# A fused linear-attention and MLP kernel: the loads of ScalarE's Gelu table are no longer written by hand

## The chip, the cores and the metric

The kernel runs on one core of a Trainium2 chip. A core has five engines with a queue each: TensorE (PE, matrix products into PSUM), ScalarE (ACT, activation functions and copies), VectorE (DVE, elementwise work), GpSimd (POOL) and SyncE (SP), which here mostly start transfers. The metric is the device time of one execution in microseconds. The time shown is a median of three runs; one further execution was taken with the hardware profiler, and all rows of the trace come from that one.

## The reference

There are two parts, one behind the other. The first is a gated linear attention: a state per batch and head decays row by row with `alpha`, takes in `k` times `v`, and is read with `q`. The second is an MLP with the tanh form of Gelu over all tokens.

```python
# q, k, v, alpha: (4, 8, 768, 48), float32
for t in range(S):
    state = alpha[:, :, t, :, None] * state + np.einsum('bhd,bhe->bhde', k[:, :, t], v[:, :, t])
    y[:, :, t] = np.einsum('bhd,bhde->bhe', q[:, :, t], state)
...
# x: (3072, 384), w_in: (384, 2048), w_out: (2048, 384)
h = x @ w_in
c = np.float32(np.sqrt(2.0 / np.pi))
g = 0.5 * h * (1.0 + np.tanh(c * (h + 0.044715 * h * h * h)))
return (g @ w_out).astype(np.float32)
```

## The kernel before

The 768 rows of a sequence are cut into six chunks of 128, the four batches into two pairs. That makes twelve pieces, "pairs" in the code, each of one chunk and two batches. Every piece goes through attention and then through the MLP.

**Attention of a piece.** ScalarE takes the logarithm of alpha (`la`, line 222). TensorE sums it along the chunk with a triangular matrix (`cum`, lines 232 and 234). ScalarE makes the exponentials of the sum and of its negative (`b` and `binv`, line 249) and of the chunk's end (`bend`, line 245). DVE multiplies `q` and `k` with them (`qp`, `kp`, line 257), TensorE transposes both (`qkT_ps`, line 268), DVE copies the transposes out of PSUM (line 278; ScalarE does some of the first two pieces). TensorE multiplies them (`at`, line 290) and DVE applies the causal mask (`atm`, line 297). TensorE makes the piece's share of the state (`kv`, line 307), which DVE adds to the state (the carry, lines 322 and 324), and the output `yps` (lines 336 and 339). That is copied out as `x` by ScalarE or DVE (line 346), transposed on TensorE (line 353) and copied into `xT` by DVE (line 357).

**MLP of a piece.** Layer 1 makes sixteen tiles `hT` of 128 x 256, each from three matmuls (line 363). ScalarE takes the Gelu of each into `gT` (line 369). Layer 2 makes two tiles `acc` of 128 x 384, each from sixteen matmuls (line 377), ScalarE or DVE copies them out as `ot` (line 384), and SyncE stores them (line 389). `hT` and `acc` share four PSUM buffers (tag `ff`): the next `hT` can be computed only when an older one has gone through its Gelu or an older `acc` has been copied.

**The order.** The program is a list of tasks, each with a kind, a modelled cost per engine, a priority, its dependencies and the buffers it takes. `Scheduler.order` (lines 49 to 120) walks through modelled time and puts the task that can start first, with the smaller priority within 60 ns, on its engine. Each engine's queue runs in that order, and an instruction that waits holds up all behind it. The MLP tasks of all pieces form one stream in a fixed order; the attention of the next pieces is put between them. A few matmuls of zeros (`idle`, line 190) are put in gaps of TensorE in the first 60 us of the plan.

**The function tables.** [...] Logarithm and exponential are in the set that the kernel calls `LN_EXP = 6`, the copies need no set of their own, and the kernel calls the set for the Gelu `GELU = 0`. The planner keeps track of the set: a task that needs another one gets 1,290 ns (`W["table"]`) added to its earliest start (line 99), and `t.load` is set to the number of the set (line 117). While the instructions are written, `run` puts a load ahead of each such task with `act_set` (lines 179 to 183), so those loads have line 181 in the trace. Independently, the compiler puts in loads of its own where it finds that an activation needs one; those have the line of that activation.

The tasks `ln` and `exp` need the first set, `gelu` the second. The Gelus of a piece are kept together, and the logarithm of a later piece waits for the last of them (lines 533 to 536), so the set changes about twice per piece.

Of the kernel before, what the change touches and what calls it, by code (L numbers as in the profile page):

```python
# [11 lines left out]
LN_EXP, GELU = 6, 0  # L12
# [117 lines left out]
class _Kernel:  # L130
# [407 lines left out]
    def run(self):  # L538
        nc = self.nc
        self.tasks()  # L540
        self.act_set(LN_EXP)
        nc.vector.memset(self.zero, 0.0)  # L542
        nc.vector.memset(self.ones, 1.0)
        first = [lambda: make_upper_triangular(nc, self.ut_h, val=1.0, diag=True), lambda: make_identity(nc, self.ident)]
        for i in range(self.BUFS["la"]):
            for n in ("la", "qp", "kp"):
                nc.vector.memset(self.ring[n][i][:, :, :, self.D:64], 0.0)
        for b in range(self.B):
            for i in range(2):
                nc.vector.memset(self.state[b][i], 0.0)  # L550
        order = self.s.order()
        self.plan = order
        gap = 0
        for t in order:
            if t.load is not None:
                self.act_set(t.load)
            t.emit(t.engine)
            if t.kind == "load" and t.engine == "POOL" and first:
                first.pop(0)()
                if not first:  # L560
                    nc.vector.tensor_copy(self.ut, self.ut_h)
# [30 lines left out]
```

## Time and profile before

| | before |
|---|---|
| median of three runs | 205.69 us (204.83 to 205.86) |
| the profiled execution | 205.91 us |
| its span, first to last instruction | 204.1 us |
| TensorE, busy | 185.2 us, 91% of the span |
| ScalarE, busy | 151.0 us, 74% |
| DVE, busy | 105.6 us, 52% |
| GpSimd, busy | 61.3 us, 30% |
| table loads, line 181 | 20, together 25.7 us |
| table loads, line 369 | 10, together 12.8 us |
| granted TensorE clock, mean over the span | 0.979 |

In rows of a group, the line and engine come first, then the operation, its output and input with their shapes, and how many there were; after the first bar the busy time in us and the mean of one in ns, after the second the idle time of the engine just before them and who ended it. In rows in order of time, start and duration in us come first, and a number in square brackets is the idle time before, with the instruction that ended it. TensorE's matmuls are pipelined and their ends are modelled: the duration of a row can reach over the start of the next one. "PEclk" or a clock is the share of the full TensorE clock that was granted.

### The profile page before, as it was taken

Reading aid. Unit: us, or ns where it says so; the run is one execution under the profiler, and the core shown is the slowest. Engines: PE = TensorE matmul, PEld = TensorE weight load, DVE = VectorE, ACT = ScalarE, POOL = GpSimd, SP = SyncE. Lnnn points to the kernel's source line nnn. Section 1 sums busy time; section 2 is a strip of 40 time slices with the busy share of each in tenths; the row PEclk is TensorE's granted clock in tenths of the full one; section 3 lists DMA queues with packets and bytes.
Section 4 is the critical chain, followed back from the end, with each engine's and each line's share of the span. In section 5 each row is a group of like instructions: output and inputs, shape, how many; then the busy total and the mean of one; then the engine's idle time right before and its main releaser. Section 6 shows DMA issues by size and latency. Waiting matters only on the chain.

```text
span 204.1 us, 4664 instructions
## 1 busy us (share of the span) xinstructions
PE 185.2 (91%) x1925; PEld 133.7 (65%) x1927; DVE 105.6 (52%) x219; ACT 151.0 (74%) x317; POOL 61.3 (30%) x63
## 2 busy tenths in 40 slices
PE   7786489999899989989989989989989989989992
PEld 2343358866578667767767767767777776676861
DVE  6373642037987394494494593594593550650000
ACT  2635767971789698798798798798798888883740
POOL 7983653464655664422410510000000000000000
PEclk9999958999999999999999999999999999999998
DMA  7999999999999999997980580200200200200202
GB/s 137 166 226 172 200 202 220 177 175 238 226 221 154 182 235 186 181 244 145 161 189 2 130 181 2 80 0 3 77 0 3 77 3 0 79 3 6 75 0 77
DMA packets 37941, 24.68 MB, mean 121 GB/s; under 512 B 27904, under 2 KB 34560, under 8 KB 37920
## 3 DMA queue, kind: packets, MB, share of 16 engines
q0 software_dynamic: 32400, 19.27, 67.2%
q1 hardware_dynamic: 5520, 5.11, 8.3%
q8 instruction: 15, 0.25, 0.6%
q14 instruction: 6, 0.05, 0.1%
HBM read 25.17 MB, written 4.72 MB: 146 GB/s over the span
## 4 chain that ended last, share of the span: by engine, by line
PE 70%; ACT 16%; DMA 6%; POOL 4%; issue 1%; DVE 1%; POOLq 0%; DVEq 0%
PE acc L377 31%; PE hT L363 27%; DMA k<-in_k_dram 6%; ACT L369 6%; ACT L181 6%; PE at L290 2%; PE yps L339 2%; ACT ot L384 2%; ACT gT L369 2%; PE cum L232 2%; PE yps L336 2%; PE xT_ps L353 2%; POOL q L202 1%; PE qkT_ps L268 1%; PE kv L307 1%
## 5 line engine op out<-in xcount | busy, mean ns | idle before, releaser
L363 PE MATMUL hT<-xT,w_in 128*128 128x256 bf16 x576 | 74.9, 278 | 8.1 <-ACT gT L369 7.9
L377 PE MATMUL acc<-w_out,gT 128*128 128x384 bf16 x384 | 68.4, 326 | 0.0
L369 ACT ACTIVATE gT<-hT 128x256 bf16<-128x256 f32 x192 | 62.0, 388 | 6.1 <-PE hT L363 5.6
L363 PEld LDWEIGHTS <-w_in 128*128 128x128 bf16 x576 | 54.6, 99 | 17.5 <-issue 9.4
L377 PEld LDWEIGHTS <-gT 128*128 128x128 bf16 x384 | 36.0, 98 | 20.4
L297 DVE TENSOR_TENSOR atm<-at,ut 128x512 bf16<-128x512 f32 x48 | 30.8, 684 | 8.1 <-PE at L290 7.0
L257 DVE TENSOR_TENSOR qp<-q,b 128x768 bf16<-128x768 f32 x12 | 11.5, 958 | 32.8 <-ACT b L249 32.8
L181 ACT ACT_TABLE_LOAD x20 | 25.7, 1283 | 1.1 <-PEq L576 0.7
L384 ACT COPY ot<-acc 128x384 f32<-128x384 f32 x18 | 8.6, 478 | 16.9 <-PE acc L377 16.7
L202 POOL DMA_DIRECT2D v<-in_v_dram x12 | 13.8, 1153 | 17.6 <-PE xT_ps L353 9.7
L346 ACT CAST x<-yps 128x384 bf16<-128x384 f32 x22 | 10.5, 478 | 11.5 <-PE yps L339 11.3
L202 POOL DMA_DIRECT2D a<-in_alpha_dram x11 | 12.7, 1153 | 20.7 <-ACT la L222 13.4
L278 DVE COPY qkT<-qkT_ps 128x1024 bf16<-128x1024 bf16 (+1 forms) x21 | 13.3, 673 | 7.6 <-PE qkT_ps L268 7.6
L357 DVE COPY xT<-xT_ps 128x384 bf16<-128x384 bf16 x24 | 8.5, 356 | 16.6 <-PE xT_ps L353 16.5
L202 POOL DMA_DIRECT2D q<-in_q_dram x12 | 14.0, 1163 | 9.9 <-DVE qp L257 4.2
L202 POOL DMA_DIRECT2D k<-in_k_dram x12 | 13.8, 1152 | 4.8 <-DVE stmp L322 2.3
L249 ACT ACTIVATE b<-cum 128x768 bf16<-128x768 f32 x12 | 9.7, 810 | 7.4 <-PE cum L234 7.4
L222 ACT ACTIVATE la<-a 128x768 f16<-128x768 f32 x12 | 10.1, 843 | 4.1 <-DMA a<-in_alpha_dram 4.0
L369 ACT ACT_TABLE_LOAD x10 | 12.8, 1283 | 0.1
L257 DVE TENSOR_TENSOR kp<-k,binv 128x768 bf16<-128x768 f32 (+1 forms) x14 | 11.6, 837 | 2.4 <-DMA k<-in_k_dram 2.4
L190 PE MATMUL idle<-zero 128*128 128x512 bf16 x37 | 11.3, 432 | 1.3 <-DVE zero L542 1.2
L324 DVE TENSOR_TENSOR st<-stmp,bend 64x192 bf16<-64x192 f32 x32 | 11.3, 353 | 1.7
(43 smaller groups left out, 167.2 us busy)
## 6 DMA issues: line engine op xcount, KB each, us to landing
q<-in_q_dram POOLq DMA_DIRECT2D x12, 384.0 KB, 12.6
k<-in_k_dram POOLq DMA_DIRECT2D x12, 384.0 KB, 12.7
out_dram<-ot SPq DMA_DIRECT2D x24, 192.0 KB, 1.9
a<-in_alpha_dram POOLq DMA_DIRECT2D x11, 384.0 KB, 12.6
v<-in_v_dram POOLq DMA_DIRECT2D x12, 192.0 KB, 12.6
w_in<-in_moe_w_in_dram POOLq DMA_DIRECT2D x4, 384.0 KB, 10.1
w_out<-in_moe_w_out_dram POOLq DMA_DIRECT2D x4, 384.0 KB, 14.7
a<-in_alpha_dram SPq DMA_DIRECT2D x1, 384.0 KB, 4.1
```

The costliest lines, as they stand in the source:

```text
L181: nc.scalar.add_instruction(mybir.InstLoadActFuncSet(name=nc.get_next_instruction_name(), act_func_set_id=i, engine=mybir.EngineType.Activ ...
L190: self.nc.tensor.matmul(ps, self.zero[:, 0:self.C], self.zero, start=True, stop=True)
L202: (nc.sync if e == "SP" else nc.gpsimd).dma_start(t.rearrange("t b h d -> t (b h) d"), src)
L257: self.nc.vector.tensor_tensor(u[n + "p"][:, lo:hi, :, 0:self.D], u[n][:, lo:hi], u["b" if n == "q" else "binv"][:, lo:hi], op=ALU.mult)
L278: self.copy(e)(t, u.pop(("T_ps", i, which)))
L297: self.nc.vector.tensor_tensor(u["atm", i][:, o], u["at", i][:, o], self.ut[:, None, :].to_broadcast([self.C, self.H // 2, self.C]), op=AL ...
L324: nc.vector.tensor_tensor(new[ps, :, fs], acc, u["bend"][ps, i, :, None].to_broadcast([64, H // 2, D]), op=ALU.mult)
L346: self.copy(e)(x, u["y", i].rearrange("t h d -> t (h d)"))
L363: self.nc.tensor.matmul(h, self.w_in[:, j, nt * self.C:(nt + 1) * self.C], self.xT[c][:, j, lo:hi].rearrange("p g t -> p (g t)"), start=j ...
L369: return lambda e: self.nc.scalar.activation(self.gT[c % self.NG][:, nt, lo * self.C:hi * self.C], f.pop(("h", c, lo, nt)), AF.Gelu_apprx_ ...
L377: self.nc.tensor.matmul(f["acc", c, b], self.gT[c % self.NG][:, nt, b * self.C:(b + 1) * self.C], self.w_out[:, nt, :], start=nt == 0, sto ...
L384: self.copy(e)(f["ot", c, b], f.pop(("acc", c, b)))
```

## The change

In the loop of `run`, a load is now written only where the task that follows needs the Ln/Exp set. The load ahead of the first Gelu of a stretch is not written any more. The load at the very start (line 541) stays. Two assignments that nothing reads, `self.plan` and `gap`, go as well. The planner, the costs that it uses, the buffers and the transfers are not touched.

```diff
@@ -549,11 +549,9 @@
             for i in range(2):
                 nc.vector.memset(self.state[b][i], 0.0)
         order = self.s.order()
-        self.plan = order
-        gap = 0
         for t in order:
-            if t.load is not None:
-                self.act_set(t.load)
+            if t.load == LN_EXP:
+                self.act_set(LN_EXP)
             t.emit(t.engine)
             if t.kind == "load" and t.engine == "POOL" and first:
                 first.pop(0)()
```

## The prediction

> **What bounds the kernel now.** I read the page of the profile first (the load on each engine, then the costliest groups), then the list of who waits for whom, and then the instructions in order of time around the table loads, ScalarE (ACT) beside TensorE (PE).
>
> ```profile
> span 204.1 us, 4664 instructions
> PE 185.2 (91%) x1925; PEld 133.7 (65%) x1927; DVE 105.6 (52%) x219; ACT 151.0 (74%) x317; POOL 61.3 (30%) x63
> ...
> L181 ACT ACT_TABLE_LOAD x20 | 25.7, 1283 | 1.1 <-PEq L576 0.7
> ...
> L369 ACT ACT_TABLE_LOAD x10 | 12.8, 1283 | 0.1
> ```
>
> TensorE is busy for 91% of the span, so whatever is done on ScalarE can give at most what TensorE now waits for. There are thirty table loads. Twenty carry line 181, the loads written by hand: one at the start, ten for Gelu, nine back to Ln/Exp. Ten more carry line 369, the Gelu activation itself, where the kernel writes no load: the compiler puts those in. So each change to Gelu is paid twice. The next view is the list of waits, the row of TensorE waiting for ScalarE's Gelu:
>
> ```profile
> PE hT L363 <- ACT gT L369: 7.9, 9, 2.1
> ```
>
> Of the 18.9 us in which TensorE is not busy (204.1 - 185.2), 7.9 us in nine waits are for the first Gelu output of a stage. Here is one steady stage, ScalarE in order of time (start, duration, line), then TensorE:
>
> ```profile
> 85.49 0.48 ACT L384 COPY ot<-acc 128x384 f32<-128x384 f32 x1 [0.39 <-PE acc L377]
> 85.98 1.28 ACT L181 ACT_TABLE_LOAD   x1
> 87.27 1.28 ACT L369 ACT_TABLE_LOAD   x1
> 88.57 2.50 ACT L369 ACTIVATE gT<-hT 128x256 bf16<-128x256 f32 x8
> ...
> 92.47 0.48 ACT L346 CAST x<-yps 128x384 bf16<-128x384 f32 x1
> ```
>
> ```profile
> 87.16 0.49 PE L363 MATMUL hT<-xT,w_in 128*128 128x256 bf16 x3
> 87.67 0.40 PE L290 MATMUL at<-qkT 64*128 64x128 bf16 x8
> 88.00 0.34 PE L307 MATMUL kv<-v,kp 128*128 128x96 bf16 x4
> 89.00 0.49 PE L363 MATMUL hT<-xT,w_in 128*128 128x256 bf16 x3 [0.66 <-ACT gT L369]
> 89.33 0.33 PE L307 MATMUL kv<-v,kp 128*128 128x96 bf16 x4
> 89.50 1.15 PE L363 MATMUL hT<-xT,w_in 128*128 128x256 bf16 x9
> ```
>
> The four hT buffers in PSUM (tag `ff`) are full, the fifth hT needs the first Gelu, and that stands behind two loads. TensorE waits 0.66 us, although the loads together are 2.56 us: most of them is covered by the matmuls at 87.16 to 88.34.
>
> **The change part by part.** It takes away the ten hand-written Gelu loads; ten loads at line 369 and ten at line 181 should be left. ScalarE loses 10 x 1.283 = 12.8 us of work. The list of tasks, its order, the buffers and all transfers stay: the planner ran before with one load of 1,290 ns per change and does so still. The two assignments that go (`self.plan`, `gap`) make no instruction.
>
> The price of one load is read from starts: 85.98 to 87.27 is 1.29, 87.27 to 88.57 is 1.30, so a load costs its 1.283 us and nothing after it, and it starts 0.01 us after the copy before it. [...]
>
> With every first Gelu 1.28 us earlier, what does TensorE gain in each stage? It gains no more than its wait. The wait as listed counts from the modelled end of the matmul before; by starts it is longer. Four kv matmuls take 89.33 to 89.50 = 0.17 before the next one starts, so the waiting hT could have started at 88.00 + 0.17 = 88.17, not at 89.00: 0.83. The Gelu will release it at 89.00 - 1.28 = 87.72, which is 0.45 before TensorE gets there, so all 0.83 goes. Five stages (85.98, 101.04, 116.09, 131.14, 146.20) are alike: 5 x 0.83 = 4.15. The others:
>
> ```profile
> 73.05 0.49 PE L363 MATMUL hT<-xT,w_in 128*128 128x256 bf16 x3
> 74.12 1.14 PE L363 MATMUL hT<-xT,w_in 128*128 128x256 bf16 x9 [0.57 <-ACT gT L369]
> ...
> 162.93 0.40 PE L290 MATMUL at<-qkT 64*128 64x128 bf16 x8
> 164.27 1.80 PE L363 MATMUL hT<-xT,w_in 128*128 128x256 bf16 x15 [0.94 <-ACT gT L369]
> ```
>
> At 74.12: three hT take 0.33 by starts (89.00 to 89.33), so 73.38 was possible: 0.74. At 164.27: eight `at` take 0.33 (87.67 to 88.00), so 163.26 was possible: 1.01, and the stage that starts at 176.13 is the same, 1.00. Both lie under 1.28. The eight stages give 0.74 + 4.15 + 2.01 = **6.90 us**. Their lower bound is the listed idle time, 0.57 + 5 x 0.66 + 2 x 0.94 = 5.75.
>
> One change to Gelu gives nothing, the one at 55.31:
>
> ```profile
> 56.59 1.28 ACT L369 ACT_TABLE_LOAD   x1
> 57.89 0.66 ACT L369 ACTIVATE gT<-hT 128x256 bf16<-128x256 f32 x2
> ```
>
> ```profile
> 57.14 0.82 PE L363 MATMUL hT<-xT,w_in 128*128 128x256 bf16 x6
> ```
>
> Its hT only starts at 57.14 and TensorE has no Gelu wait there; I cost it at 0. It also shows that the compiler's load doesn't wait for the matmul as its activation does: it began at 56.59. So the load left over takes the removed one's place in time.
>
> The first change to Gelu needs care, because of the clock:
>
> ```profile
> 23.33 1.28 ACT L181 ACT_TABLE_LOAD   x1
> 24.61 1.28 ACT L369 ACT_TABLE_LOAD   x1
> 25.91 1.66 ACT L369 ACTIVATE gT<-hT 128x256 bf16<-128x256 f32 x5
> ```
>
> ```profile
> 23.69 0.52 PE L307 MATMUL kv<-v,kp 128*128 128x96 bf16 x8
> 26.34 0.80 PE L363 MATMUL hT<-xT,w_in 128*128 128x256 bf16 x3 [2.13 <-ACT gT L369]
> ```
>
> Stretches of TensorE by their granted clock (from:to, length, busy, clock, share of the DMA engines, GB/s):
>
> ```profile
> 25.00:25.10 0.10, 0.00 (x0) 0.63 1.31 205
> ...
> 31.80:31.90 0.10, 0.10 (x5) 0.73 1.44 388
> ...
> 202.50:203.00 0.50, 0.00 (x0) 0.52 0.00 0
> ```
>
> Here the wait is longer than a load, so TensorE restarts at 26.34 - 1.28 = 25.06 and still waits about a microsecond, from 23.69 + 2 x 0.17 = 24.03 to 25.06. The clock halves at 25.03 (0.63 over that tenth of a microsecond) and comes back at 31.85. From 26.34 to 31.85 TensorE works without a break at half clock: 5.51 us for 2.76 us of full-clock work. What the earlier restart is worth depends on when the clock returns, which the trace of before can't show. Bounds: it returns at 31.85 as before, and 25.06 to 31.85 holds 6.79 / 2 = 3.40 of work instead of 2.76: 0.64 gained. Or it never drops, because the gap is shorter: 1.28 + 2.76 = 4.04. Between: the three changes of the clock, 25.03, 31.85 and 202.52, lie 6.82 and 170.67 apart, 2 and 50 steps of 3.41. If the clock is judged at such steps, the first step of the slow stretch (25.03 to 28.44) held 1.31 of idle time and was not enough, and the second (28.44 to 31.85), busy throughout, was. With the restart at 25.06 already the first is full, and the clock returns at 28.44: 3.38 / 2 = 1.69 of the work is done by then, the other 1.07 by 29.51 instead of 31.85: **2.34 us**. I take this, since the whole of the first step is then like the whole of the second; the drop itself at 25.03 lies before the new restart, and nothing before it changes.
>
> [...]
>
> **What could be late next.** DVE, in the steady stages, and the loads in the first third:
>
> ```profile
> 90.52 0.35 DVE L324 TENSOR_TENSOR st<-stmp,bend 64x192 bf16<-64x192 f32 x1
> 91.01 1.29 DVE L297 TENSOR_TENSOR atm<-at,ut 128x512 bf16<-128x512 f32 x2
> ...
> 92.96 0.36 DVE L322 TENSOR_TENSOR stmp<-kv,st 64x192 f32<-64x192 f32 x1
> ```
>
> ```profile
> 94.56 0.33 PE L336 MATMUL yps<-st,qkT 128*128 128x96 bf16 x4
> ```
>
> ```profile
> 45.52 0.85 ACT L222 ACTIVATE la<-a 128x768 f16<-128x768 f32 x1
> 49.41 0.48 ACT L384 COPY ot<-acc 128x384 f32<-128x384 f32 x1 [3.05 <-PE acc L377]
> ```
>
> DVE is busy until 90.52 + 0.35 = 90.87, so the masks at 91.01 and the carry behind them can come only 0.14 earlier, while TensorE comes 0.83 earlier. The next y (94.56) needs the carry's read of kv (ends 93.32): 94.56 - 0.83 = 93.73 against 93.18, a reserve of 0.55. I cost it at 0. The Ln at 45.52 is the one whose input may land too late once TensorE is some 2 us ahead, but behind it ScalarE has 3.05 us of idle time, so this too is 0. The Ln/Exp load and its Ln follow the y matmuls of the same stage and move with TensorE.
>
> **The sum.** The profiled execution took 205.91 us (204.1 span and 1.8 around it), 0.22 above the median of 205.69, so inside the spread of the three runs (204.83 to 205.86 is 1.03 wide). 205.91 - 6.90 - 2.34 = 196.67, say **196.7 us**, 4.4% under the median. With the lower bounds 205.91 - 5.75 - 0.64 = 199.5; with the upper ones 205.91 - 6.90 - 4.04 = 195.0.
>
> **The rivals.**
>
> The slow clock lasts as long as before. Then the first change gives 0.64: 205.91 - 6.90 - 0.64 = 198.4. For it: steps of 6.82 fit the three changes of the clock as well (1 and 25). and a clock judged at other moments in another execution could do the same. Against: the stretch from 28.44 to 31.85, without a pause, is more than enough of a busy step, and the new first half equals it. Chance 0.26.
>
> Another wait takes over: the carry binds y. That needs the reserve of 0.55 to be gone, for instance if y waits for the carry's end rather than its read. At worst DVE lets six stages (74 to 149) gain 0.14 each instead of 0.74 to 0.83, 4.05 less: 196.7 + 4.05 = 200.7. Chance 0.06.
>
> All nine removed loads on the chain count in full:
>
> ```profile
> PE 70%; ACT 16%; DMA 6%; POOL 4%; issue 1%; DVE 1%; POOLq 0%; DVEq 0%
> PE acc L377 31%; PE hT L363 27%; DMA k<-in_k_dram 6%; ACT L369 6%; ACT L181 6%; PE at L290 2%; PE yps L339 2%; ACT ot L384 2%; ACT gT L369 2%; PE cum L232 2%; PE yps L336 2%; PE xT_ps L353 2%; POOL q L202 1%; PE qkT_ps L268 1%; PE kv L307 1%
> ```
>
> The chain has line 181 with 6%, about nine times 1.28 = 11.5 us: 205.91 - 11.5 = 194.4. Against: beside the loads TensorE has its own work, and a chain shorter by 1.28 hands over to it after 0.83. Chance 0.05.
>
> A removed load frees more than its own 1.283 us. If a wait after it went too, the first change would lose its whole pause (24.03 to 26.34, 2.31) and with it the slow clock, 2.76: 205.91 - 6.90 - 5.07 = 193.9. No row shows such a wait. Chance 0.03. [...]
>
> Nothing is removed: the hand-written load was what let the compiler do with one, and it places two now. The time stays at 205.9. Against: its load at line 369 begins 0.01 us behind the hand-written one and is the last before the Gelu, so it pays no heed to it. Chance 0.03.
>
> Slower: without the hand-written load the compiler chooses a set for the Gelu stretch that lacks the copy of `x` (line 346, at 92.47 between the Gelus), and loads twice around it, 2.57 us. TensorE runs ahead of ScalarE by the four hT buffers, 4 x 0.33 = 1.31, so 1.26 of it is lost; the time is worse than before from 9.24 / 1.26 = 7.3 such places on. With one in each of the nine stages 196.7 + 11.3 = 208.0. Against: the set in use there is already the compiler's own choice and the copies run without a load. Chance 0.03.
>
> **How the numbers follow.** The forecast has 0.54; its own range, from the bounds of the eight waits and of small shifts of the clock's steps, is 196.0 to 198.0. The range for 8 in 10 takes in the rival of the clock and most of the way to the bounds: 195.2 to 199.2. A difference of under 0.5% (1.0 us, the spread of the three runs) can't be told from no change. Faster than that are the forecast and the first four rivals, 0.94; the same, 0.03; slower, 0.03.
>
> **What would show it.** Line 181 with ten loads, line 369 with ten; ScalarE 12.8 us less busy. No Gelu wait of TensorE in the stages from 71 us on, and those stages shorter by 0.74 to 1.0. One wait of about 0.9 us near 24, then half clock for 3.4 us instead of 6.8. Wrong would be: loads at other lines; waits of TensorE for DVE at `yps` in place of the Gelu ones; a slow stretch that still ends near 31.9 or doesn't occur.

## The result, and the profile after

The changed kernel takes 197.60 us (median of four runs, 195.95 to 198.04), the kernel before 205.78 (204.83 to 205.93): a ratio of 0.9597 with a 95% interval of 0.9534 to 0.9661, 8.2 us less. The forecast was 196.7, its range 195.2 to 199.2. The profiled execution of the changed kernel took 195.95 us with a span of 194.2, the fastest of the four.

The page of the changed kernel: engines, chain, and the groups with the loads.

```profile
span 194.2 us, 4654 instructions
PE 184.1 (95%) x1925; PEld 133.1 (69%) x1927; DVE 105.7 (54%) x219; ACT 139.7 (72%) x307; POOL 61.4 (32%) x63
...
PE 84%; DMA 6%; POOL 4%; ACT 2%; DVE 1%; issue 1%; POOLq 0%; DVEq 0%
...
L181 ACT ACT_TABLE_LOAD x10 | 12.8, 1283 | 0.9 <-PEq L574 0.7
...
L369 ACT ACT_TABLE_LOAD x10 | 12.8, 1283 | 0.2
```

Ten loads are gone, and they are those of line 181. ScalarE's share of the chain falls from 16% to 2%: TensorE is now followed back nearly without a break. ScalarE lost 11.3 us of busy time and not 12.8, because the 192 Gelus are busy for 1.4 us longer (63.4 instead of 62.0): Gelus that stand back to back overlap (eight took 2.50 us at 88.57 in the kernel before, where one takes 0.38), and ScalarE now waits for an hT between them 19 times instead of 15.

The same steady stage as in the prediction, ScalarE and then TensorE in order of time, and TensorE's only wait for a Gelu in the whole program:

```profile
81.54 0.48 ACT L384 COPY ot<-acc 128x384 f32<-128x384 f32 x1 [0.39 <-PE acc L377]
82.04 1.28 ACT L369 ACT_TABLE_LOAD   x1
83.33 1.21 ACT L369 ACTIVATE gT<-hT 128x256 bf16<-128x256 f32 x4
```

```profile
84.05 0.34 PE L307 MATMUL kv<-v,kp 128*128 128x96 bf16 x4
84.23 0.49 PE L363 MATMUL hT<-xT,w_in 128*128 128x256 bf16 x3
84.56 0.33 PE L307 MATMUL kv<-v,kp 128*128 128x96 bf16 x4
```

```profile
PE hT L363 <- ACT gT L369: 0.8, 1, 0.8
```

The hT that waited now starts 0.18 after the kv matmuls before it. To see where the time went, the same instruction is looked up in both traces, first in the kernel before, then in the changed one: the start of the first layer 2, of a `cum` in three later stages, and of the last-but-one long run of layer 2. "Ahead by" in the table behind them is the start in the kernel before less the start in the changed one.

```profile
39.22 3.41 PE L377 MATMUL acc<-w_out,gT 128*128 128x384 bf16 x20
82.81 0.32 PE L232 MATMUL cum<-la,ut_h 128*128 128x384 f16 x1
158.08 0.32 PE L232 MATMUL cum<-la,ut_h 128*128 128x384 f16 x1
172.96 0.33 PE L232 MATMUL cum<-la,ut_h 128*128 128x384 f16 x1
184.59 5.36 PE L377 MATMUL acc<-w_out,gT 128*128 128x384 bf16 x32
```

```profile
36.01 3.41 PE L377 MATMUL acc<-w_out,gT 128*128 128x384 bf16 x20
78.87 0.32 PE L232 MATMUL cum<-la,ut_h 128*128 128x384 f16 x1
150.02 0.32 PE L232 MATMUL cum<-la,ut_h 128*128 128x384 f16 x1
163.90 0.33 PE L232 MATMUL cum<-la,ut_h 128*128 128x384 f16 x1
174.64 5.36 PE L377 MATMUL acc<-w_out,gT 128*128 128x384 bf16 x32
```

| up to | ahead by | gained there | the prediction's term |
|---|---|---|---|
| 39.22 | 3.21 | 3.21 | 2.34 for the first change |
| 82.81 | 3.94 | 0.73 | 0 for the change near 55, 0.74 for the next |
| 158.08 | 8.06 | 4.12 in five stages | 4.15 |
| 172.96 | 9.06 | 1.00 | 1.01 |
| 184.59 | 9.95 | 0.89 | 1.00 |

Behind 184.59 nothing changes. The first 39 us gave more than the term, and a part of that isn't due to the change. TensorE's wait for `kp`, which stands behind a transfer of k (DVE begins `kp` when that has landed, at 21.67 before and 20.78 after), and the first Gelu, first before, then after:

```profile
22.29 0.87 PE L268 MATMUL qkT_ps<-ident,kp 128*128 128x128 bf16 x8 [1.25 <-DVE kp L257]
```

```profile
21.40 0.86 PE L268 MATMUL qkT_ps<-ident,kp 128*128 128x128 bf16 x8 [0.63 <-DVE kp L257]
...
24.16 0.80 PE L363 MATMUL hT<-xT,w_in 128*128 128x256 bf16 x3 [0.85 <-ACT gT L369]
```

The transposes of k start 0.89 earlier in this execution, ahead of any Gelu. Without that 3.21 - 0.89 = 2.32 is left for the first change. The clock of TensorE in the changed kernel, by tenths of a microsecond:

```profile
24.10:24.20 0.10, 0.04 (x1) 0.72 1.27 200
27.50:27.60 0.10, 0.10 (x2) 0.72 1.35 207
```

It fell at 24.14 and came back at 27.56, 3.42 us later; in the kernel before the slow stretch was 6.82 us long (25.03 to 31.85). One step of 3.4 us stands in place of two. That is the case on which the 2.34 was worked out. But the other three runs of the changed kernel have a mean clock of 0.983, 0.979 and 0.978 instead of 0.991, and took 197.3 to 198.0. That is the mean of two slow steps: the kernel before, with two, has 0.979, in which a slow stretch behind its last matmul counts too (from 202.52 to the end at 204.1). Whether that explains the 0.9 us between forecast and median was the first question for the experiments.

### The profile page after: what moved, and what is told of

Read it like the earlier page. It is cut to its first block, busy times and chain, and to the rows that moved or that the text cites. A ratio compares the mean times of both kernels' runs of the same rounds, so it can differ in the third digit from the quotient of the medians.

```text
span 194.2 us, 4654 instructions
## 1 busy us (share of the span) xinstructions
PE 184.1 (95%) x1925; PEld 133.1 (69%) x1927; DVE 105.7 (54%) x219; ACT 139.7 (72%) x307; POOL 61.4 (32%) x63
## 4 chain that ended last, share of the span: by engine, by line
PE 84%; DMA 6%; POOL 4%; ACT 2%; DVE 1%; issue 1%; POOLq 0%; DVEq 0%
PE hT L363 33%; PE acc L377 32%; DMA k<-in_k_dram 6%; PE qkT_ps L268 5%; PE at L290 4%; PE yps L339 2%; PE kv L307 2%; PE xT_ps L353 2%; PE cum L232 2%; PE yps L336 2%; POOL q L202 1%; PE cum L234 1%; POOL w_in L210 1%; DVE kp L257 1%; ACT L369 1%
## 5 line engine op out<-in xcount | busy, mean ns | idle before, releaser
L363 PE MATMUL hT<-xT,w_in 128*128 128x256 bf16 x576 | 73.8, 275 | 1.1 <-ACT gT L369 0.8
L369 ACT ACTIVATE gT<-hT 128x256 bf16<-128x256 f32 x192 | 63.4, 386 | 8.5 <-PE hT L363 7.3
L363 PEld LDWEIGHTS <-w_in 128*128 128x128 bf16 x576 | 53.7, 98 | 9.4 <-issue 1.7
L257 DVE TENSOR_TENSOR qp<-q,b 128x768 bf16<-128x768 f32 x12 | 11.5, 958 | 33.1 <-ACT b L249 33.1
L190 PE MATMUL idle<-zero 128*128 128x512 bf16 x37 | 12.4, 468 | 1.3 <-DVE zero L542 1.2
L181 ACT ACT_TABLE_LOAD x10 | 12.8, 1283 | 0.9 <-PEq L574 0.7
L369 ACT ACT_TABLE_LOAD x10 | 12.8, 1283 | 0.2
L324 DVE TENSOR_TENSOR st<-stmp,bend 64x192 bf16<-64x192 f32 x32 | 11.3, 353 | 1.7
## 6 DMA issues: line engine op xcount, KB each, us to landing
out_dram<-ot SPq DMA_DIRECT2D x24, 192.0 KB, 1.9
v<-in_v_dram POOLq DMA_DIRECT2D x12, 192.0 KB, 12.9
```

The lines of the kernel that those rows point to most:

```text
L181: nc.scalar.add_instruction(mybir.InstLoadActFuncSet(name=nc.get_next_instruction_name(), act_func_set_id=i, engine=mybir.EngineType.Activ ...
L190: self.nc.tensor.matmul(ps, self.zero[:, 0:self.C], self.zero, start=True, stop=True)
L257: self.nc.vector.tensor_tensor(u[n + "p"][:, lo:hi, :, 0:self.D], u[n][:, lo:hi], u["b" if n == "q" else "binv"][:, lo:hi], op=ALU.mult)
L324: nc.vector.tensor_tensor(new[ps, :, fs], acc, u["bend"][ps, i, :, None].to_broadcast([64, H // 2, D]), op=ALU.mult)
L363: self.nc.tensor.matmul(h, self.w_in[:, j, nt * self.C:(nt + 1) * self.C], self.xT[c][:, j, lo:hi].rearrange("p g t -> p (g t)"), start=j ...
L369: return lambda e: self.nc.scalar.activation(self.gT[c % self.NG][:, nt, lo * self.C:hi * self.C], f.pop(("h", c, lo, nt)), AF.Gelu_apprx_ ...
```

## The experiments

The theory: a stage gains what TensorE waited there and no more (6.90 us in eight stages), and the first change gives something between 0.64 and 4.04, by how the slow stretch of the clock falls. The rivals: every removed load on the chain counts in full; the gain is mainly one of the clock; a load by hand is dear in itself. All times below are medians, with the kernel before run on the same chip beside them.

### The load back at the first change only

```diff
             if t.load == LN_EXP:
                 self.act_set(LN_EXP)
+            elif t.load == GELU:
+                changes += 1
+                if changes == 1:
+                    self.act_set(GELU)
```

> The hand-written Gelu load is put back ahead of the first change to Gelu alone, so the first change is as in the kernel before and the other nine are as in the changed kernel. My account (a stage gains its wait and no more): 205.8 - 6.90 = 198.9, between 197.9 and 199.9 as the slow clock falls; stages of 14.23 us in place of 15.05. The rival that every removed load on the chain counts in full: 205.8 - 8 x 1.28 = 195.5. The rival that nearly all came from the slow clock near 25 us: about 204.

Measured: 198.76 against 205.62, ratio 0.966 (0.9613 to 0.9706). The nine changes behind the first give 6.86 us by the medians; the term was 6.90. The interval leaves room for 6.0 to 8.0, so the agreement to 0.04 is luck, and the tighter test of the term is the sum of the differences in the traces above, 0.73 + 4.12 + 1.00 + 0.89 = 6.74. The rival that counts the loads, 195.5, lies outside the interval (197.7 to 199.6), and so does the one by the clock alone. In the profiled execution (199.27 us) the first pause is back, 1.6 us, and the only Gelu wait left:

```profile
PE hT L363 <- ACT gT L369: 1.6, 1, 1.6
```

### The load back at all changes but the first

```diff
-                if changes == 1:
+                if changes > 1:
```

> The hand-written Gelu load is put back ahead of all changes but the first. My account: the first change alone gives 0.64 (slow clock as long as before) to 2.34 (one step shorter): 203.5 (202.4 to 205.2). Together with the kernel that has it only at the first change this should make up the whole gain of 8.2: 6.9 there and 1.3 to 2.3 here.

Measured: 204.18 against 205.15, ratio 0.9932 (0.9901 to 0.9963). The first change alone gives 0.97 us by the medians and 1.4 by the ratio, with an interval of 0.8 to 2.0. Its twelve runs spread from 201.69 to 204.86, and the mean clock goes with them: 201.7 and 202.0 at 0.998 and above, 203.2 at 0.992, 203.5 to 204.3 at 0.983, 204.5 to 204.9 at 0.980. Two slow steps are the common case, and in it the first change gives about 1 us. By the medians 6.86 + 0.97 = 7.83; the whole change gave 8.18 in its first runs, 7.90 and 8.38 in the two repeats below.

### The changed kernel again, twice

> The changed kernel again. My account: its runs fall in groups by how long the slow clock lasts near 24 us, one step of 3.4 us (195.9 as in the profiled execution, clock 0.991) or two (198, clock 0.979), with up to 0.9 us more by when the transfer of k lands; nothing between the stages of 71 and 190 us moves. If the spread comes from elsewhere, the clock of the runs doesn't go with their span.

> The changed kernel beside the kernel with added matmuls, on the same chip: 197.2, clock 0.983 in most runs (two steps of the slow clock).

Measured: 197.25 (195.45 to 198.00) against 205.15, and 197.17 (196.63 to 197.97) against 205.55; ratios 0.9611 (0.9573 to 0.9649) and 0.9601 (0.9574 to 0.9628). All sixteen runs of the changed kernel fall into groups by mean clock:

| mean clock | runs | time |
|---|---|---|
| 0.991 to 0.998 | 3 | 195.45 to 196.63 |
| 0.983 | 8 | 196.92 to 197.57 |
| 0.978, 0.979 | 5 | 197.73 to 198.04 |

Two steps of 3.41 us at half clock (0.50 in the rows below) in 195.5 us are a mean clock of 1 - 3.41 / 195.5 = 0.983. So the execution that was profiled first, with one step, is one of the rare ones; the usual one has two. The traces of the two repeats bear this out: the one with a mean of 0.998 has no slow step near 24 us (1.00 from 18 to 35), the one with 0.983 has two. Here are the two (from:to, length, busy, clock), and TensorE's first wait for a Gelu in the same execution:

```profile
23.15:26.56 3.41, 3.08 (x30) 0.50 1.29 203
26.56:29.97 3.41, 3.41 (x24) 0.50 1.31 203
```

```profile
24.82 0.80 PE L363 MATMUL hT<-xT,w_in 128*128 128x256 bf16 x3 [0.33 <-ACT gT L369]
```

Here the clock fell at 23.15, ahead of the wait. The first slow step holds the wait, and a second one followed. In the execution with one step the clock fell at 24.14, when the wait was all but over (24.16).

### Matmuls of zeros in the pauses, in both kernels

Ahead of the transposes of q, of those of k and of kv of the second piece, TensorE gets work whose results nobody reads, where it waits in any case.

```diff
+            second = u is self.p[0, 1] and i == 0
+            if second and which == "q":
+                idle = self.tile("yk", [C, 512], F32, "idle")
+                for _ in range(4):
+                    nc.tensor.matmul(idle, self.zero[:, 0:C], self.zero, start=True, stop=True)
...
+            for _ in range(6 if second and which == "k" else 0):
+                nc.tensor.transpose(ps[:, 0, 0, :], self.ident, self.ident)
...
+            for _ in range(5 if u is self.p[0, 1] and i == 0 else 0):
+                nc.tensor.matmul(kv.rearrange("t p d -> t (p d)"), self.zero[:, 0:C], self.zero[:, 0:4 * 2 * D],
+                                 start=True, stop=True)
```

> The changed kernel with matmuls of zeros and transposes that nobody reads in the pauses of TensorE in the attention of the second piece: four of 512 columns ahead of the transposes of q, six transposes of 128 ahead of those of k, five of 384 columns ahead of kv, at places where TensorE waits anyway. My account: the slow clock near 24 to 28 us (or to 31 us in other executions) is due to these pauses; without it 1.7 us are gained against the profiled execution of the changed kernel and up to 3.4 against its slower ones: 194.4 (193.5 to 195.5), clock 0.99 or more over the span, and a narrower spread of the runs. If the slow clock has another cause, or the added matmuls cost what they gain: 197.6.

> The kernel before with the same added matmuls. My account: 205.8 less what the slow clock cost, 2.76: 203.0 (202 to 204). With the clock out of the way in both, the change is worth 6.90 in the eight stages and 1.28 in the first, 8.2 us, between this kernel and the changed one with the same matmuls. If the difference between the two is 9.2 or more, the clock is not what made the first stage's gain uncertain; if 6.9 or less, the first stage gives nothing.

Measured: 195.38 for the changed kernel (195.24 to 196.71), 203.36 for the kernel before (202.91 to 203.63), beside 205.15. The pauses do cause most of the slow stretch: with them filled, four of six runs of the changed kernel have a clock of 0.999 or 1.000, which none of its sixteen runs had without, and it gains 1.9 us; the kernel before gains 1.8. It isn't gone altogether: four of the six runs of the kernel before still have 0.988 or 0.989 (203.3 to 203.6 us, against 202.9 and 203.2 at 1.000), and where the slow time lies in these was not recorded. Between the two kernels with filled pauses lie 7.98 us; 6.90 + 1.28 = 8.18 was expected. In the other two runs of the changed kernel the clock fell all the same (0.988 and 0.991, 196.6 and 196.7). One of these, the second, was profiled: the clock fell at 23.99 and was 0.50 up to 27.40, the five matmuls ahead of kv took 1.51 us instead of the 0.99 of the traced kernel before with the same matmuls (at 1.00), and the hT behind them began 1.03 us after the start of the first Gelu (24.60), where in the first repeat it was 0.43:

```profile
23.68 1.51 PE L314 MATMUL kv<-zero 128*128 128x384 bf16 x5
24.98 0.85 PE L317 MATMUL kv<-v,kp 128*128 128x96 bf16 x8
25.63 0.84 PE L373 MATMUL hT<-xT,w_in 128*128 128x256 bf16 x3
```

### The added matmuls, placed better

```diff
-            for _ in range(6 if second and which == "k" else 0):
-                nc.tensor.transpose(ps[:, 0, 0, :], self.ident, self.ident)
+            if second and which == "k":
+                idle = self.tile("ca", [C, 2, 512], F32, "idle")
+                for _ in range(3):
+                    nc.tensor.matmul(idle[:, 0], self.zero[:, 0:C], self.zero, start=True, stop=True)
...
-            for _ in range(5 if u is self.p[0, 1] and i == 0 else 0):
+            for _ in range(3 if u is self.p[0, 1] and i == 0 else 0):
```

> The changed kernel with added matmuls of zeros in the same pauses, moved: four of 512 columns ahead of the transposes of q, three of 512 ahead of those of k (in the place of six transposes), three of 384 ahead of kv (in the place of five). The first try left the slow clock in two of six runs, and where it came, the five matmuls ahead of kv ran at half clock and held up the next hT. My account: 195.3, clock 0.998 or more in most runs, none above 196.7. If the added matmuls delay the transposes of k: 195.8.

Measured: 195.26 us, and all five runs between 195.06 and 195.35; beside it the changed kernel 197.17 and the kernel before 205.55. The ratio to the kernel before is 0.9507 (0.9485 to 0.9529). This version beats both kernels, and its runs agree within 0.3 us where those of the changed kernel spread by 1.3. Their mean clocks are 0.988 to 1.000; the run with 0.988 took 195.35. TensorE in order of time:

```profile
19.51 0.81 PE L269 MATMUL idle<-zero 128*128 128x512 bf16 x3
20.35 0.62 PE L277 MATMUL qkT_ps<-ident,qp 128*128 128x128 bf16 x8
20.81 0.81 PE L273 MATMUL idle<-zero 128*128 128x512 bf16 x3
22.00 0.87 PE L277 MATMUL qkT_ps<-ident,kp 128*128 128x128 bf16 x8 [0.39 <-DVE kp L257]
23.08 0.40 PE L299 MATMUL at<-qkT 64*128 64x128 bf16 x8 [0.21 <-ACT qkT L287]
23.41 0.66 PE L316 MATMUL kv<-zero 128*128 128x384 bf16 x3
23.90 0.50 PE L319 MATMUL kv<-v,kp 128*128 128x96 bf16 x8
24.77 0.49 PE L375 MATMUL hT<-xT,w_in 128*128 128x256 bf16 x3 [0.36 <-ACT gT L381]
```

Of the four ahead of q the trace holds three. No useful matmul starts later for them: waits for `kp` and for the Gelu are left behind the added work. The clock stays at 1.00 from 18 to 35 us in this execution.

### All loads by hand, with the right number

```diff
-LN_EXP, GELU = 6, 0
+LN_EXP, GELU = 6, 11
...
-            if t.load == LN_EXP:
-                self.act_set(LN_EXP)
+            if t.load is not None:
+                self.act_set(t.load)
```

> All Gelu loads are written by hand again as in the kernel before, but with the number 11 in place of 0 for the Gelu set. If the double load came only from a set that doesn't hold the tanh form of Gelu, the compiler adds none: twenty loads at line 181, none at line 369, and the time of the changed kernel, 197.6 (196 to 198.2). If a load by hand costs by itself, or the compiler adds its own in any case: 205.8.

Measured: 197.14 (196.65 to 197.72), ratio 0.9597 (0.9561 to 0.9633), the changed kernel's. The group with the loads is now the only one:

```profile
L181 ACT ACT_TABLE_LOAD x20 | 25.7, 1283 | 1.1 <-PEq L574 0.7
```

So the double load of the kernel before was a wrong number. With 0 the compiler put a load of its own behind each of the ten (line 369, ten loads); with 11 it added none.

### No loads by hand

```diff
-            if t.load == LN_EXP:
-                self.act_set(LN_EXP)
```

> Only the load at the very start is written by hand; the Ln/Exp loads are left to the compiler too. The program then has 28 loads: the compiler takes one set for Ln and another for Exp, so nine more loads stand between a Ln (line 222) and its first Exp (line 249). My account: of that load 0.75 us is covered, since ScalarE waits for cum there; b comes about 0.54 later, kp has a reserve of some 0.09 before TensorE wants it, so each of eight stages loses about 0.45: 197.6 + 3.6 = 201.2 (200 to 203). Each load in full, 8 x 1.28: 207.9. If the extra loads are covered altogether: 197.6.

Measured: 202.32 (202.01 to 202.61), ratio 0.9839 (0.9808 to 0.9871), 5.1 us above the changed kernel in its repeats. Ten loads stand between a Ln and its Exp, 31 in all (the expectation's 28 was a miscount). From the page, then a stage on ScalarE and TensorE:

```profile
L222 ACT ACT_TABLE_LOAD x10 | 12.8, 1283 | 0.2
L249 ACT ACT_TABLE_LOAD x10 | 12.8, 1283 | 0.2
L369 ACT ACT_TABLE_LOAD x10 | 12.8, 1283 | 0.2
```

```profile
97.24 1.28 ACT L249 ACT_TABLE_LOAD   x1
98.53 0.81 ACT L249 ACTIVATE b<-cum 128x768 bf16<-128x768 f32 x1
```

```profile
100.73 0.39 PE L268 MATMUL qkT_ps<-ident,qp 128*128 128x128 bf16 x4
101.26 0.40 PE L268 MATMUL qkT_ps<-ident,kp 128*128 128x128 bf16 x4
```

The four transposes of qp take 0.22 by starts (as between the transposes elsewhere), so those of kp start 0.31 late. The account had 0.45 for each of eight stages, 3.6 in all; the stages lose about 0.3, 2.5 in all. Of the other 2.6, 1.3 come from a place that the account had left out, a copy of `x` near 55 us that stands behind an added load and makes TensorE wait 1.84 us instead of 0.55; the rest was not followed up. The Ln/Exp load by hand, which the change keeps, is worth these 5 us.

### One load more per change

```diff
+            elif t.load == GELU:
+                for _ in range(2):
+                    self.act_set(GELU)
```

> Two hand-written Gelu loads per change in place of the one of the kernel before, three with the compiler's. Nothing covers the added load in the nine stages where TensorE already waits: 9 x 1.28, and at the change near 55 us, where before there is a reserve of about 0.96, 0.3 more: 205.8 + 11.9 = 217.7, up to 2 more if the longer first pause lengthens the slow clock. If loads in a row overlap, or a switch to the set already there is cheap: under 210. [...]

Measured: 205.48 against 205.62, ratio 0.9993 (0.9969 to 1.0016). This answers nothing about the price of a load: the trace has twenty loads at line 181, not thirty. The second load of a set that is there already was not executed; what left it out, these runs don't show. So the kernel ran as before, and the test had to be made with two different sets:

```diff
-                for _ in range(2):
-                    self.act_set(GELU)
+                for i in (GELU, 1):
+                    self.act_set(i)
```

> As the kernel before, with one more hand-written load per change to Gelu, of yet another set (0, then 1, then the compiler's), so that three loads of three sets stand in a row; the earlier try had the same set twice, and only one of the two was in the program. The added load is covered nowhere in the nine stages where TensorE already waits, 9 x 1.28 = 11.5, and costs 0.3 at the change near 55 us, where before there is a reserve of about 0.96: 205.4 + 11.9 = 217.3, up to 2 more if the longer first pause lengthens the slow clock. [...] If a load is worth to TensorE only the 0.83 us that a stage gained when one went: 205.4 + 7.5 = 212.9.

Measured: 223.54 (223.47 to 225.43) against 205.55, ratio 1.0907 (1.0867 to 1.0948): 18.0 us slower, where 11.9, up to 13.9 with a longer slow clock, was expected. ScalarE and TensorE of a stage, and the wait:

```profile
89.93 2.57 ACT L181 ACT_TABLE_LOAD   x2
92.51 1.28 ACT L369 ACT_TABLE_LOAD   x1
```

```profile
94.24 0.49 PE L363 MATMUL hT<-xT,w_in 128*128 128x256 bf16 x3 [1.95 <-ACT gT L369]
```

```profile
PE hT L363 <- ACT gT L369: 19.2, 10, 2.9
```

The waits behaved as the account has it. Each load takes 1.28 or 1.29 with nothing behind it, TensorE's wait in a steady stage goes from 0.66 to 1.95, and all waits together from 7.9 to 19.2, 11.3 more. The other 6.7 us go with the clock: TensorE's 1925 matmuls are busy for 192.0 us instead of 185.2, 6.8 more. Stretches of TensorE, with the granted clock behind the busy time:

```profile
76.00:80.00 4.00, 3.47 (x22) 0.57 1.44 235
110.00:115.00 5.00, 4.42 (x33) 0.66 0.41 74
144.00:149.00 5.00, 4.15 (x31) 0.66 0.00 0
178.00:183.00 5.00, 3.91 (x32) 0.66 0.00 0
```

Four new slow stretches of one step each (3.41 us), 34 us apart, in stages where the clock of the kernel before was 1.00 (31.9 to 202 us). At half clock 4 x 3.4 us cost at most 6.8, less what TensorE waited in them; the first slow stretch, from 21.9 to 32.1, lasted three steps here. How the 6.7 divide between these was not measured. The expectation had at most a longer first slow stretch, and came out 6 us too low.

## Why the prediction was right, point by point

**What is removed.** Ten loads went, line 369 kept its ten, and the load left over starts where the removed one did, 0.02 us after the copy before it. As forecast.

**The price of a load, 1.283 us with nothing behind it.** It held: in the kernel with three sets the loads start 1.29 us apart, and a steady stage's wait grew by 1.29. The rival of a hidden wait behind each load is excluded by these rows: the next activation starts 1.29 to 1.30 us after the start of its load in every stage shown.

**Eight stages, 6.90 us.** Right to 0.2 us: 0.73, 4.12, 1.00 and 0.89 in the traces, 6.74 together; 6.86 measured by leaving the first change alone. Reading the wait by starts, 0.83 rather than the 0.66 printed in the row, was right: the printed idle time begins at a modelled end, and the sum of the printed ones, 5.75, would have been 1.0 us short. Only the last stage gave 0.11 less than its term. There a copy of `x` on ScalarE, which the transposes of `x` wait for, began 0.74 us after the start of the `yps` matmuls ahead of it (172.08), instead of 0.46 in the kernel before (181.85); why is not known.

**The reserves.** The carry's 0.55, and the late Ln at 45.52, were enough: no new wait of TensorE for DVE appeared in the stages. The rival in which the carry takes over did not come.

**The first change, 2.34 us.** The course was right, and the case was too good. In the profiled execution everything came as worked out: one slow step of 3.42 us, 2.32 us gained. But the rival of the slow clock itself left room for other moments in another execution, and they mostly come: thirteen of sixteen runs have a mean clock of 0.983 or less, two steps. Measured alone, the first change gives 0.97 us. The step of 3.41 us itself was borne out: the slow stretches near 24 us in the traces are about 3.41, 6.82 or 10.24 us long. That the clock is judged by what TensorE did in such a step was the author's estimate, and no run shows it directly.

The number of slow steps differs between executions of the kernel before too: of the 41 runs beside the experiments one has a mean clock of 0.992 (one step), 28 have 0.979 or 0.983 (two), and twelve 0.975 or less (three, as in the trace with 0.971 of the kernel with the load back at the first change). So 2.34 compares an execution of the kernel before that had two slow steps with one of the changed kernel that had one. Compared at the same number of steps, from the start of the transposes of `kp` to the start of the first layer 2, the traces say:

| slow steps | as before | changed | gained |
|---|---|---|---|
| none | 14.40 (with filled pauses) | 13.10 | 1.30 |
| one | 15.63 (with the load written twice) | 14.61 | 1.02 |
| two | 16.93 | 15.47 | 1.46 |

The first change is worth about its load of 1.28 us, and the rest of the 2.34 is one slow step less. That one is had only where the steps happen to lie well. So the term that was mis-sized is this one, 2.34 instead of 1.0 to 1.5, and the place where it failed is the choice of the value inside the bounds (0.64 to 4.04) from one phase of the clock's steps, that of the profiled execution. The reason given for the choice, that a step busy throughout ends the slow stretch, held in every trace (none near 24 us went on behind a step that was busy for all of its 3.41 us); but how much less than throughout is enough stays open: in the kernel with the load written twice a step that was busy for 2.84 of 3.41 us ended it, and one with 3.08 in the changed kernel's trace with two steps did not. With 1.0 and the medians of the kernel before (205.15 to 205.78), 7.9 less is 197.2 to 197.9, and the medians measured are 197.17 to 197.60. In its course the rival that the slow clock lasts as long as before (0.64, 198.4, at a chance of 0.26) is the usual run. In time the medians lie between it and the forecast, since in the traced run with two steps the clock fell ahead of the wait (23.15), and what it slowed there cost nothing: the wait shrank from 0.85 to 0.33 us, and the hT behind it started 2.77 us after the transposes of `kp`, as against 2.76 with one step.

**What the profiled execution shows beyond that.** Its 195.95 has 0.89 us from a transfer of k that landed earlier, which no term has, since it isn't of the change. That this execution comes within 0.7 us of the forecast is in part luck.

**The rivals by the chain.** The chain had 6% for line 181, 11.5 us. The kernel with the load back at the first change excludes that each counts in full: by that rival it would have taken 195.5, and it took 198.76.

## What to carry to other kernels

Take a wait from the starts of the instructions around it, stage by stage, and let no stage gain more than that: here this gave 6.90 for 6.74 in the traces, where the loads counted in full, 8 x 1.28, give 10.3. Count table loads by line in the trace, since those written by hand with a wrong number were paid here beside the compiler's (8 us), while with none by hand the compiler switched ten times between Ln and Exp, which ran without a switch behind the load by hand (5 us). And where the matmul clock dips in a profiled execution, look at several runs' mean clocks before building a term on the place of the dip; ten matmuls in pauses where the engine waits anyway took most of the dip away here (mean clocks of 0.988 to 1.000), for 1.0%.

## What the runs showed of the hardware that had not been expected

A pause of about 2 us was enough in four of eight stages to halve TensorE's clock, although the stages are otherwise busy: with three loads in a row the pause is 1.86 to 2.23 us, and these four slowed for one step of 3.4 us each, where with pauses of 0.57 to 0.94 us in the kernel before the clock stayed at 1.00 from 31.9 to 202 us. The steps lay differently from one execution to the next: in the changed kernel's traces the clock fell at 24.14 us, at 23.15, and not at all between 18 and 35, and its times spread by 2.6 us in sixteen runs; with ten matmuls in the pauses five runs agreed within 0.3 us. How busy TensorE was just before did not tell by itself when the clock fell: it fell behind 3.41 us of which 2.05 were busy (the first try with filled pauses) and stayed at 1.00 in the first repeat, where of the 3.41 us from 20.0 on only 1.63 were busy.

A second load of the set just loaded was left out: with ten pairs of set 0 and ten other loads written, twenty were executed at that line. A load by hand with a number of no use to the Gelu was executed all the same, 1.28 us each, and a set that served the next function was taken: set 0 was followed by another load each of ten times, and sets 6 and 11 were not.
